# Joins of the 32-row inverses as products of two units, an fp32 second product in the small expert slots, and a new order table

## The chip, the core and the metric

The kernel runs on one core of a Trainium2 chip. The metric is the device time of one execution in microseconds (us). The core has five instruction queues that run side by side, each in its own order: PE (TensorE, the matrix products; its weight loads are counted apart as PEld), DVE (VectorE), ACT (ScalarE), POOL (GpSimd) and SP (SyncE, which here issues most transfers). An instruction that waits holds back everything behind it on its engine. A lower share of busy time on one engine says little by itself: the program has stages with different limits.

## What is computed

Three layers follow one another. The first is a delta-rule attention over 768 positions, for 32 units (4 batches of 8 heads, 48 wide):

```
for t in range(S):
    y[:, :, t] = einsum('bhd,bhde->bhe', q[:, :, t], state)
    v_old = einsum('bhde,bhd->bhe', state, k_n[:, :, t])
    state = state + beta * einsum('bhd,bhe->bhde', k_n[:, :, t], v - v_old)
```

Its output, 3072 rows of 384, goes into a layer of eight experts: each row picks the expert with the largest logit, and gets `gate * (relu(x @ w1[e]) @ w2[e])`, with 1024 hidden columns. The third layer is a gated network on all rows: `h = x @ w_in`, `g = h * sigmoid(h)`, `out = g @ w_out`, with 2048 hidden columns.

## The kernel before

**Attention.** Time is cut into six chunks t of 128 positions, each into two halves e of 64, each of these into two blocks of 32 rows; units come in two groups p of 16. Within 64 rows the recurrence is solved with the inverse of a triangular matrix. Its two diagonal 32-row blocks are inverted for all units at once on DVE: `to_lanes` transposes the Gram blocks (L354), `norms` and `scales` make the factors, `step` (L404, L410 and their neighbours) does 31 dependent elimination steps, and `spread` (L420) transposes the result back. From there PE joins the two 32-row inverses to one of 64 rows: `join` (px, L435) and `turn_upper` (pt, L444), each 32 products of 32x32 per chunk and group, both copied by ACT (`keep_join`), and `lower` (po, L456), 32 more. Then follow `weigh` (L472, L473), `update` (L489), `state` (L505), `read` (L519), the transposes of the output (L786) and the router's logits (L802, L810). State goes from half to half and from chunk to chunk, so that these run in a chain. The Gram products are L329, the eviction of the masked ones is L340.

**Router.** After chunks 2 and 5 a pass on DVE and PE (`rank`, `finish`, L837 to L1100) ranks the rows, places them in slots and makes the index lists. Group 0 has five small slots of 256 rows, from the first half of the positions; group 1 four regular slots of 512 rows.

**Small slots.** A slot goes through 8 hidden blocks c of 128 columns. For each, the weights are split into a rounded part and a remainder (ACT L1280, DVE L1283, both for w1 and for w2), the first product takes nine matmuls of 256 columns (L1226), ACT applies the relu and writes its rounded part (L1317), DVE writes the remainder (L1320), and the second product takes three matmuls of 384 columns for each of two row blocks (L1233 with out `po`). 5 slots of 8 blocks make 40 such steps.

**Regular slots and the third layer** do the same with 512 rows (L1226 with out `ph`, L1233 with out `poe`) and then with L1609 and L1626. While the expert slots run, DVE and ACT also unpack the third layer's 64-bit weights (L1498 to L1507).

**What sets the order.** Attention, router and small slots are one list of jobs. `Order.solve` gives each job a rank, from a table of numbers (`PLAN["rank"]`) and the planned cost of what depends on it, and builds one order for each engine from planned costs and dependences; `emit` writes the instructions in that order and puts dummy products (L683, "pulses") where PE would stand idle. Regular slots and third layer are written after that; the framework interleaves them.

Of the kernel before, what the change touches and what calls it, by code (L numbers as in the profile page):

```python
# [22 lines left out]
    one=3,  # L23
    rank=dict(
        kq=-239.1, qb=147.9, vs=127, kd=578.4, gr=546.9, gq=-202.8, Gc=-247.9, Kc=160.5, dg=-13.6, zero=-244.4,
        L=237.9, sc=-13.3, b2=167.7, ln=-189.8, va=362.8, st=401, sp=462.8, ga=-851.5, px=-535.6, pt=359.1, X=-283.4,
        T=525.1, po=127.7, o=117.8, w=565, wc=-96.5, up=-260.7, uc=474.7, ps=-321.1, sc2=659.4, py=-453, Y=991.4,
        out=-12.8, xt=177.8, xc=6.6, gt=105.9, wv1=989.6, wv2=209.6, wv4=522, wv5=388.1, one=278.9, kz=21.8,
        ask=332.1, gates=-98.2, val=689.8, fe=-28.1, xg=10, tr=535.4, th=-20.7, tl=267.6, s1h=609, s1l=111.9,
        s2h=215, s2l=68.5, fi=-316.7, rh=-579, rl=-41.6, se=540, ev=-129.8, ys=-3.2, kq0=-193.7, kq1=316, kq2=167.9,  # L30
        kq3=-402.6, kq4=441.9, kq5=-347.4, qb0=-385.7, qb1=-50.8, qb2=270.9, qb3=-148, qb4=236.9, qb5=-273.3,
        vs0=-154.6, vs1=389.7, vs2=-687.6, vs3=-414.5, vs4=516.3, vs5=-50, kd0=303.3, kd1=243.7, kd2=-122.1,
        kd3=237.6, kd4=27.8, kd5=11.9, gr0=311.6, gr1=332.7, gr2=448.3, gr3=593, gr4=92.4, gr5=585.6, gq0=110.8,
        gq1=142.8, gq2=257.1, gq3=485.4, gq4=128.6, gq5=8.9, Gc0=-90.3, Gc1=-187.1, Gc2=154.7, Gc3=494.8, Gc4=-106.5,
        Gc5=-286.8, Kc0=-237.1, Kc1=305.5, Kc2=207.8, Kc3=125.8, Kc4=-357.2, Kc5=-175.8, dg0=69.1, dg1=-574.4,
        dg2=-256.8, dg3=12, dg4=405.5, dg5=273, zero0=-54, zero1=-452.2, zero2=-377.7, zero3=-404.9, zero4=-41.9,
        zero5=-0.1, L0=-107.8, L1=120.6, L2=-181.8, L3=894.2, L4=387.6, L5=-525.1, sc0=449.4, sc1=-48.2, sc3=1031.7,
        sc4=-89.2, sc5=-268.2, b20=445.1, b21=-23.3, b22=-42.7, b23=-277.3, b24=-397.4, b25=-376.7, ln0=586.1,
        ln1=226.1, ln2=790.8, ln3=324.6, ln4=-521.3, ln5=-62.2, va0=516.2, va1=587.4, va2=604.8, va3=122.6,
        va4=-545.8, va5=680.5, st0=-244.5, st1=-650, st2=149.7, st3=-98.4, st4=109.9, st5=136.7, sp0=318.8, sp1=-397,  # L40
        sp2=-105, sp3=-270.1, sp4=332.3, sp5=246.3, ga0=664.7, ga1=135.6, ga2=281.1, ga3=-382.8, ga4=6.3, ga5=405.9,
        px0=-343.9, px1=122.6, px2=997.5, px3=512.2, px4=33.2, px5=250, pt0=820.3, pt1=-209.9, pt2=78.9, pt3=356.1,
        pt4=442, pt5=73.3, X0=103.8, X1=18.1, X2=-31, X3=135.3, X4=290.9, X5=28.6, T0=326.2, T1=6.3, T2=323.9,
        T3=178.2, T4=-45.6, T5=159.7, po0=92.1, po1=425, po2=-537.7, po3=4.5, po4=151.8, po5=1075.1, o0=5.3,
        o1=156.3, o2=487.5, o3=-9.3, o4=-4.3, o5=-172.3, w0=512.1, w1=543.7, w2=-613.9, w3=555.4, w4=-341.1, w5=17.4,
        wc0=-524.6, wc1=370.4, wc2=162.5, wc3=-396.4, wc4=132.4, wc5=43.8, up0=-144.5, up1=-17, up2=17.1, up3=404.2,
# [4 lines left out]
        out5=136.5, xt0=354.1, xt1=-244.1, xt2=-557.6, xt3=-21.9, xt4=-596.7, xt5=-3.3, xc0=137.4, xc1=587,  # L51
        xc2=-418.9, xc3=325.9, xc4=111.8, xc5=320.6, gt0=-54.3, gt1=1.7, gt2=74.9, gt3=48.9, gt4=135.4, gt5=-396.6,
    ), half=161.8,
    ex=146.6, n0=40, npre=40, tok=70,
)


# [1756 lines left out]
```

## Time and profile before

| | us |
|---|---|
| median of 3 runs | 971.99 |
| lowest and highest | 971.89, 973.62 |
| the profiled execution | 972.41 |
| its span on the core | 970.7 |

The span is what the trace covers; 1.7 us of the execution lie around it. The page gives PE as busy for 905.5 us (93%), weight loads 796.6 (82%), DVE 608.1 (63%), ACT 439.2 (45%), POOL 84.6 (9%). These are means over four stages that differ: attention up to about 296 us, small slots up to about 410, regular slots up to about 561, and the third layer. A table of the busy time of each engine by stage is the view to begin with. A busy PE is not a PE at its peak: dummy products count, and a matmul counts as busy while its pipeline fills. How far apart matmuls start tells what they cost in a dense run.

### The profile page before, as it was taken

How to read it: one execution, taken by the hardware profiler on the slowest of the kernel's cores; microseconds unless marked ns; L12 is line 12 of the kernel's file. 1: busy time of each engine (PE TensorE's matmuls, PEld its weight loads, DVE VectorE, ACT ScalarE, POOL GpSimd, SP SyncE). 2: the span in 40 equal slices, each digit the busy share in tenths (PEclk: the TensorE clock that was granted, in tenths of full speed). 3: DMA queues.
4: the chain of work that ended last, by engine and by line, in shares of the span. 5: the costliest groups of instructions: out<-in, count | busy, mean ns of one | idle time of the engine just before them, and what ended most of it. 6: DMA issues, size and time to landing. Idle time of an engine off the chain costs nothing. (4 is left out here: it accounts for less than half of the span.)

```text
span 970.7 us, 26047 instructions
## 1 busy us (share of the span) xinstructions
PE 905.5 (93%) x10897; PEld 796.6 (82%) x10897; DVE 608.1 (63%) x1724; ACT 439.2 (45%) x868; POOL 84.6 (9%) x85
## 2 busy tenths in 40 slices
PE   7779797898989888999998999999999999999997
PEld 4458686776879887788997999989999899999997
DVE  5999599679958999999643466533334333333332
ACT  4036373645866556756443454433323332332322
POOL 5000000000001213424211010000000000000000
PEclk8888897988979999999998999999999999999999
DMA  9942654445434533857541322001001000000000
GB/s 187 191 119 65 140 114 109 104 104 118 93 88 148 150 97 129 264 179 241 179 131 53 98 68 82 6 28 33 33 1 33 33 1 1 33 1 1 33 1 33
DMA packets 76273, 85.44 MB, mean 88 GB/s; under 512 B 38153, under 2 KB 62871, under 8 KB 76144
## 3 DMA queue, kind: packets, MB, share of 16 engines
q1 hardware_dynamic: 72816, 73.83, 28.8%
q0 software_dynamic: 3328, 9.83, 3.0%
q8 instruction: 88, 1.44, 0.7%
q14 instruction: 41, 0.34, 0.1%
HBM read 70.53 MB, written 14.55 MB: 88 GB/s over the span
## 5 line engine op out<-in xcount | busy, mean ns | idle before, releaser
L1626 PE MATMUL fpo<-o,fgh 128*128 128x384 f32 x768 | 184.3, 338 | 0.0
L1614 DVE TENSOR_TENSOR fy<-fph,fy 128x512 f32<-128x512 f32 x96 | 66.4, 692 | 161.4 <-ACT fy L1612 161.0
L1626 PEld LDWEIGHTS fpo<-o,fgh 128*128 128x128 f32 x768 | 139.3, 188 | 7.9 <-ACT fgh L1616 0.4
L1612 ACT ACTIVATE fy<-fph 128x512 f32<-128x512 f32 x96 | 57.5, 598 | 169.0 <-PE fph L1609 166.1
L1626 PE MATMUL fpo<-o,fgl 128*128 128x384 f32 x384 | 116.6, 338 | 0.0
L1609 PE MATMUL fph<-fxh,ih 128*128 128x512 f32 x288 | 113.7, 395 | 0.0
L1609 PE MATMUL fph<-fxl,ih 128*128 128x512 f32 x288 | 113.3, 394 | 0.0
L1618 DVE TENSOR_TENSOR fgl<-fy,fgh 128x512 fp32r<-128x512 f32 x96 | 66.5, 692 | 74.7 <-ACT fgh L1616 64.3
L1609 PE MATMUL fph<-fxh,il 128*128 128x512 f32 x288 | 113.2, 393 | 0.0
L1616 ACT CAST fgh<-fy 128x512 fp32r<-128x512 f32 x96 | 59.7, 622 | 80.6 <-DVE fy L1614 44.6
L1233 PE MATMUL poe<-wKT,pairs 128*128 128x384 f32 x384 | 76.5, 344 | 4.0 <-ACTq L1470 3.1
L1233 PEld LDWEIGHTS poe<-wKT,pairs 128*128 128x128 f32 x384 | 69.0, 192 | 7.4 <-ACTq L1470 3.4
L1626 PEld LDWEIGHTS fpo<-o,fgl 128*128 128x128 f32 x384 | 71.1, 188 | 0.5
L404 DVE TENSOR_TENSOR tmp<-A,L 128x126 f32<-128x126 f32 (+20 forms) x336 | 70.7, 252 | 0.8
L410 DVE TENSOR_TENSOR A<-A,tmp 128x126 f32<-128x126 f32 (+20 forms) x336 | 70.5, 251 | 0.0
L683 PE MATMUL po<-dense 128*128 128x512 bf16 x163 | 55.4, 457 | 14.4 <-DVE KB L340 5.3
L1233 PE MATMUL po<-wKT,hs 128*128 128x384 f32 x240 | 54.7, 355 | 11.1 <-DVE wKT L1283 6.8
L1609 PEld LDWEIGHTS fph<-fxl,ih 128*128 128x128 f32 x288 | 54.1, 188 | 10.5
L1609 PEld LDWEIGHTS fph<-fxh,il 128*128 128x128 f32 x288 | 54.1, 188 | 9.7
L1609 PEld LDWEIGHTS fph<-fxh,ih 128*128 128x128 f32 x288 | 54.1, 188 | 9.0
L1233 PEld LDWEIGHTS po<-wKT,hs 128*128 128x128 f32 x240 | 40.4, 193 | 16.2 <-DVE wKT L1283 8.8
L1226 PE MATMUL bank<-xh,wRH 128*128 128x256 f32 x240 | 51.5, 291 | 0.9 <-DVE wRH L1283 0.8
(435 smaller groups left out, 1594.5 us busy)
## 6 DMA issues: line engine op xcount, KB each, us to landing
raw<-in_moe_w_dram SPq DMA_DIRECT2D x72, 384.0 KB
ri<-in_moe_w_in_dram SPq DMA_DIRECT2D x12, 512.0 KB
ro<-in_moe_w_out_dram SPq DMA_DIRECT2D x16, 384.0 KB
vs<-in_vd_dram SPq DMA_DIRECT2D x12, 384.0 KB
KI<-in_kd_dram SPq DMA_DIRECT2D x24, 192.0 KB
Z<-vs SPq DMA_DIRECT2D x24, 192.0 KB
xs<-Y SPq DMA_DIRECT2D x48, 96.0 KB
fy<-ys SPq DMA_DIRECT2D x6, 768.0 KB
```

The source lines that it names most:

```text
L404: nc.vector.tensor_tensor(tv, r[:, :, j : j + 1].to_broadcast([128, c, n]), L[:, j : j + 1, j + 1 :].to_broadcast([128, c, n]), op=ALU.mult,)
L410: nc.vector.tensor_tensor(r[:, :, j + 1 :], r[:, :, j + 1 :], tv, op=ALU.add)
L683: return nc.tensor.matmul(room, dense, dense[:, None, :].to_broadcast([128, 4, 128]), start=True, stop=True).ins
L1226: self.nc.tensor.matmul(ph, a[:, k, :], b[:, k, :], start=(i == 0), stop=(i == 8))
L1233: self.mark = self.nc.tensor.matmul(o, a[:, cs], b, start=(c == 0 and i == 0), stop=(c == self.F - 1 and i == 2)).ins
L1609: nc.tensor.matmul(ph, a[:, k, fs], b[:, k, :], start=(n == 0), stop=(n == 8))
L1612: nc.scalar.activation(sg, ph, AF.Sigmoid)
L1614: nc.vector.tensor_tensor(gv, ph, sg, op=ALU.mult)
L1616: self.marks = [nc.scalar.copy(gh, gv).ins]
L1618: self.marks.append(nc.vector.tensor_tensor(gl, gv, gh, op=ALU.subtract).ins)
L1626: nc.tensor.matmul(po[c], a[:, rows], b, start=(f == 0 and i == 0), stop=(f == 15 and i == 2))
```

## The change

It has four parts.

**Joins.** `join`, `turn_upper` and `lower` take two neighbouring units in one product, with 64 columns in the left factor. px then holds all four 32x32 products of a pair; the copy of pt is written twice by ACT, each time multiplied by a column of zeros and ones (`halves`), so that the left factor of po is block-diagonal. 16 products stand where 32 stood. The buffer G is laid out so that the blocks to be inverted lie together.

**Small slots.** The second product reads the relu's output and w2 as plain fp32, one matmul per row block. The split of w2 and the remainder of the hidden rows are gone. The second product holds the raw w2 until it has read it.

**Buffers and dependences.** A and L have two buffers each, so a chunk's clearing and its transposition to lanes no longer wait for the chunk before; keys have five half-buffers in place of six. Steps of two chunks could be done together (`together`), for the chunks named in `pair`.

**Order.** Planned costs of PE jobs are changed, and all ranks in the table are new. Since the ranks are numbers, what they do is shown by the order below.

```diff
-    one=3,
+    one=3, pair=(),
     rank=dict(
-        kq=-239.1, qb=147.9, vs=127, kd=578.4, gr=546.9, gq=-202.8, Gc=-247.9, Kc=160.5, dg=-13.6, zero=-244.4,
+        kq=198.9, qb=242.4, vs=64.9, kd=1074.8, gr=178.8, gq=-206.4, Gc=265.8, Kc=-543.5, dg=116.5, zero=481.9,
...
-        for tag, w in (("KQ0", 3072), ("KQ1", 1024), ("RH", 1536), ("KT", 1536)):
+        for tag, w in (("KQ0", 3072), ("KQ1", 1024), ("RH", 1536)):
...
     def join(self, t, p):
+
         G = self.g(t, p)
-        px = self.st[t]["px", p] = self.bank([128, 8, 32], f"px{t}_{p}")
+        px = self.st[t]["px", p] = self.bank([128, 8, 2, 32], f"px{t}_{p}")
         for n in range(8):
-            for q in range(4):
-                e, w = divmod(q, 2)
-                r, u = slice(64 * e + 32, 64 * e + 64), 2 * n + w
-                self.nc.tensor.matmul(px[32 * q : 32 * q + 32, n], G[r, u, 0:32], G[r, u, 32:64], start=True, stop=True)
+            for e in range(2):
+                r, u = slice(64 * e + 32, 64 * e + 64), slice(2 * n, 2 * n + 2)
+                self.nc.tensor.matmul(px[64 * e : 64 * e + 64, n], G[r, 0, u].rearrange("p w c -> p (w c)"), G[r, 1, u], start=True, stop=True)
...
-        self.nc.scalar.copy(X, self.st[t]["p" + x, p])
+        if x == "x":
+            self.nc.scalar.copy(X, self.st[t]["px", p])
+        else:
+            for w in range(2):
+                self.nc.scalar.mul(X[:, :, w, :], self.st[t]["pt", p], self.halves[:, w : w + 1])
...
     def lower(self, t, p):
         X, T = self.st[t]["Xx", p], self.st[t]["Xt", p]
-        po = self.st[t]["po", p] = self.bank([128, 8, 32], f"po{t}_{p}")
+        po = self.st[t]["po", p] = self.bank([128, 8, 2, 32], f"po{t}_{p}")
         for n in range(8):
-            for q in range(4):
-                r = slice(32 * q, 32 * q + 32)
-                self.nc.tensor.matmul(po[r, n], T[r, n], X[r, n], start=True, stop=True)
+            for e in range(2):
+                r = slice(64 * e, 64 * e + 64)
+                self.nc.tensor.matmul(po[r, n], T[r, n].rearrange("p w c -> p (w c)"), X[r, n], start=True, stop=True)
...
-            add(("zero", t), "POOL", 1.0, lambda t=t: self.clear_inverses(t), [("sp", t - 1)])
+            add(("zero", t), "POOL", 1.0, lambda t=t: self.clear_inverses(t), [("sp", t - 2)])
             add(("L", t), "DVE", 1.9, lambda t=t: self.to_lanes(t),
-                [("dg", t, p, e) for p in range(2) for e in range(2)] + [("st", t - 1, 30)])
+                [("dg", t, p, e) for p in range(2) for e in range(2)] + [("st", self.together(max(t - 2, 0))[0], 30)] * (t > 1))
...
         def relu(s, c):
-            nc.scalar.activation(self.bufs["hh"][c % 2], v["ph", s, c], AF.Relu)
-
-        def rest_of(s, c):
-            nc.vector.scalar_tensor_tensor(
-                self.bufs["hl"][c % 2], v["ph", s, c], 0.0, self.bufs["hh"][c % 2], op0=ALU.max, op1=ALU.subtract
-            )
+            nc.scalar.activation(v["h"][c % 2], v["ph", s, c], AF.Relu)
 
         def second(s, c):
-            self.second(c, [x[:, 0:384] for x in self.po], *(self.bufs[x][c % 2] for x in ("hh", "hl", "h2", "l2")))
+            for b in range(2):
+                nc.tensor.matmul(
+                    self.po[b][:, 0:384], v["h"][c % 2][:, 128 * b : 128 * b + 128], self.raw(1, c),
+                    start=(c == 0), stop=(c == F - 1),
+                )
...
-                    old = [(f"s{part + 1}{x}", s - 1, c + k, 0) for x in "hl" for k in range(2)]
+                    old = [(x, s - 1, c + k, 0) for x in (("s1h", "s1l") if part == 0 else ("se",)) for k in range(2)]
```

What the new table does to the order is seen at three places. The first is DVE behind `spread` of the last chunk, before the change (L420 is the transposition, L871 to L882 and L837 to L841 are the router):

```order
L410 TENSOR_TENSOR A_4594<-A_4594,tmp_30_0_5333 128x16
L410 TENSOR_TENSOR A_4594<-A_4594,tmp_30_1_5335 128x15
L420 STREAM_TRANSPOSE G<-A_4594 128x32x32
L871 TENSOR_TENSOR rk_5371<-ranks,OH 128x64
L873 TENSOR_REDUCE r_0_5373<-rk_5371 128x8
L876 TENSOR_TENSOR ge_5375<-r_0_5373,k_131 128x192
L880 TENSOR_REDUCE pd<-ge_5375 128x8
L882 SCALAR_TENSOR_TENSOR pm<-pd,r_0_5373 128x8
L837 TENSOR_REDUCE mx_5445<-lg 128x4
L839 TENSOR_TENSOR eq_5447<-lg,mx_5445 128x32
```

Here the pass over group 0 follows the last `spread`. The same engine after the change, ahead of the steps of chunk 4 (L388 lengthens the values, L1124 and L1126 end the group's lists, L347 evicts Gram products, L361 goes to lanes, L399 and L403 begin the steps):

```order
L388 TENSOR_TENSOR vs_0_2777<-vs_0_2777,nt_3568 128x768
L1124 COPY gate_3948<-ranks 128x10
L1126 TENSOR_TENSOR gate_3948<-gate_3948,ranks 128x10 x2
L388 TENSOR_TENSOR vs_1_2936<-vs_1_2936,nt_3568 128x768
L347 TENSOR_TENSOR KB_109<-bank_128,amask 64x512 x2
L361 STREAM_TRANSPOSE L_3956<-G 128x1024
L399 TENSOR_TENSOR L_3461<-L_3461,b_4_3572 128x256
L403 SCALAR_TENSOR_TENSOR A_2419<-L_3461,A_2419 128x31
```

The whole pass over group 0, which stood behind the last `spread`, now stands ahead of the steps of chunk 4, and chunk 5's transposition to lanes (L361) ahead of them too. The second place is DVE at the end of chunk 4's steps and behind the last chunk's, after the change (L438 is `spread`, L1308 splits w1, L1335 a slot's rows):

```order
L422 TENSOR_TENSOR A_2419<-A_2419,tmp_27_1_4475 128x14x4
L1308 TENSOR_TENSOR wRH<-raw_4193,wRH 128x384
L416 TENSOR_TENSOR tmp_28_0_4490<-A_2419,L_3461 128x45
...
L438 STREAM_TRANSPOSE G<-A_2419 128x32x32
L1308 TENSOR_TENSOR wRH<-raw_4193,wRH 128x384
L373 RECIPROCAL rn_4528<-n_5_4014 128x32
...
L438 STREAM_TRANSPOSE G<-A_3272 128x32x32
L1308 TENSOR_TENSOR wRH<-raw_4193,wRH 128x384 x2
L388 TENSOR_TENSOR vs_0_3527<-vs_0_3527,nt_4533 128x768
```

Before the change no split of expert weights stood ahead of the last `spread`; now seven do. The third place is PE at the last chunk's joins, before the change (bank is a PSUM bank):

```order
L810 MATMUL bank_121<-ident,xT_0_5174 128x128
L435 MATMUL bank_122<-G 32x32 x32
L435 MATMUL bank_123<-G 32x32 x32
L444 MATMUL bank_119<-ident,G 32x32 x32
L444 MATMUL bank_120<-ident,G 32x32 x32
L683 LDWEIGHTS dense
L683 MATMUL po_170<-dense 128x512
```

and after it (L453 px, L461 pt, L480 po, L543 `read`, L1252 the first product of a small slot):

```order
L453 MATMUL bank_127<-G 64x64 x16
L461 MATMUL bank_128<-ident,G 64x32 x16
L453 MATMUL bank_124<-G 64x64 x16
L543 MATMUL bank_125<-Z_112,KB_108 64x48 x16
L480 MATMUL bank_126<-Xx_0_5184,Xt_0_5205 64x64 x16
L461 MATMUL bank_127<-ident,G 64x32 x16
L1252 MATMUL bank_128<-xh_4351,wRH 128x256
L1252 MATMUL bank_128<-xl_4352,wRH 128x256
```

A matmul of a small slot stands where a dummy product stood. Seven of the 40 steps of the small slots now stand ahead of the last chunk's px on PE, about ten more between the products of its tail. Dummy products fall from 163 to 103.

## Rows read from the trace of the kernel before

**Rows 1.** Busy time by stage: stretch, length, busy (count) by engine, granted clock, DMA.

```profile
core 0: us, PE busy (x) PEld busy (x) DVE busy (x) ACT busy (x) POOL busy (x), PEclk, DMA share, GB/s
138.90:178.20 39.30, 33.14 (x1029) 27.43 (x1026) 35.78 (x145) 16.76 (x37) 0.95 (x1) 0.83 0.46 102
178.20:231.80 53.60, 48.39 (x1519) 41.26 (x1515) 40.09 (x161) 33.07 (x70) 0.95 (x1) 0.90 0.52 118
231.80:262.00 30.20, 27.24 (x936) 22.01 (x925) 29.48 (x143) 20.12 (x44) 0.95 (x1) 0.89 0.41 94
262.00:286.00 24.00, 20.03 (x679) 15.61 (x681) 13.39 (x71) 13.58 (x30) 0.79 (x1) 0.79 0.36 73
296.00:410.40 114.40, 102.12 (x743) 95.40 (x744) 107.54 (x275) 70.77 (x161) 26.88 (x24) 0.97 0.46 147
410.40:560.60 150.20, 145.91 (x739) 131.28 (x739) 95.20 (x188) 75.80 (x152) 33.15 (x24) 0.98 0.46 147
560.60:970.70 410.10, 405.15 (x2059) 367.27 (x2057) 164.74 (x262) 137.05 (x234) 3.34 (x4) 1.00 0.07 25
```

**Rows 2.** The last two `spread`s on DVE, in the timeline: start, length, operation.

```profile
229.54 2.22 DVE L420 STREAM_TRANSPOSE G<-A 128x1024 f32<-128x1024 f32 x1
259.77 2.29 DVE L420 STREAM_TRANSPOSE G<-A 128x1024 f32<-128x1024 f32 x1
```

**Rows 3.** DVE's waits, 62 to 262 us: total, times, longest.

```profile
DVE KB L340 <- PE bank L329: 14.0, 8, 4.6
DVE rn L366 <- ACT n L360: 10.8, 2, 6.6
DVE lg L813 <- PE bank L810: 1.5, 1, 1.5
```

**Rows 4.** Waits of the router's pass over group 0, 262 to 296 us.

```profile
DVE rk L871 <- PE ranks L863: 7.5, 1, 7.5
DVE p1f L1077 <- PE ranks L1072: 1.5, 1, 1.5
```

**Rows 5.** Weight loads that waited for nothing shown, 62 to 296 us.

```profile
PEld bank L444 <- issue: 10.2, 4, 2.8
PEld bank L329 <- issue: 8.1, 7, 2.8
PEld bank L435 <- issue: 6.6, 5, 4.0
```

**Rows 6.** PE's timeline: 120 rows of px, 64 rows of `update`.

```profile
265.05 1.32 PE L435 MATMUL bank<-G 32*32 32x32 f32 x120
85.10 2.07 PE L489 MATMUL bank<-Z,KA 128*64 128x48 f32 x64
```

**Rows 7.** PE's timeline in a small slot: six second, nine first products, next second.

```profile
330.34 1.21 PE L1233 MATMUL po<-wKT,hs 128*128 128x384 f32 x6
331.38 0.28 PE L1226 MATMUL bank<-xh,wRH 128*128 128x256 f32 x1
...
332.45 0.52 PE L1233 MATMUL po<-wKT,hs 128*128 128x384 f32 x2
```

**Rows 8.** Chain that ended last: a run of twelve transposes of 128 fp32 columns.

```profile
549.07 1.31 PE fpt L1593 x12
```

**Rows 9.** Waits of PE and its weight loads in the small slots, 296 to 411 us.

```profile
PE po L1233 <- DVE wKT L1283: 6.8, 5, 3.0
PEld po L1233 <- DVE wKT L1283: 8.8, 7, 3.3
PEld po L1233 <- DVE hs L1320: 6.9, 9, 2.5
```

**Rows 10.** Groups by line, whole run: busy us, mean ns, idle before and releaser.

```profile
L1283 DVE TENSOR_TENSOR wKT<-raw,wKT 128x384 fp32r<-128x384 f32 x40 | 21.4, 550 | 0.9 <-ACT wKT L1280 0.8
L1320 DVE SCALAR_TENSOR_TENSOR hs<-bank,hs 128x256 fp32r<-128x256 f32 x40 | 16.6, 416 | 1.4 <-ACT hs L1317 1.3
L448 ACT COPY Xt<-bank 128x256 f32<-128x256 f32 x12 | 4.5, 373 | 15.0 <-PE bank L444 15.0
```

More of the change, by code (lines that the diff above doesn't have):

```diff
@@ L54 @@
-    ex=146.6, n0=40, npre=40, tok=70,
+        kq=198.9, qb=242.4, vs=64.9, kd=1074.8, gr=178.8, gq=-206.4, Gc=265.8, Kc=-543.5, dg=116.5, zero=481.9,
+        L=-45.2, sc=-154.7, b2=340.1, ln=213.1, va=184.7, st=-507.6, sp=-287.4, ga=-146.4, px=174.1, pt=-1057.9,
+        X=305.7, T=-753.7, po=227.7, o=-75.7, w=-47.4, wc=358.3, up=-972, uc=248.6, ps=313.7, sc2=440.7, py=-130,
+        Y=295.3, out=42.8, xt=584.3, xc=262.8, gt=-535.2, wv1=331.6, wv2=-1257.8, wv4=-528.6, wv5=1423.9, one=13,
+        kz=-116.7, ask=630.4, gates=494.4, val=-1272.9, fe=560.9, xg=-121.2, tr=351.3, th=-1084.9, tl=-543.8,
@@ L249, in __init__ @@
         nc.vector.memset(self.tiny, 1e-36)
+        self.halves = cp.tile([128, 2], F32, name="halves")
+        nc.vector.memset(self.halves, 0.0)
+        for q in range(4):
+            nc.vector.memset(self.halves[32 * q : 32 * q + 32, q % 2 : q % 2 + 1], 1.0)
         self.bl = cp.tile([128, T, 32], F32, name="bl")
-        self.G = cp.tile([128, 4, N, 64], F32, name="G")
+        self.G = cp.tile([128, 2, 2, U, 32], F32, name="G")
         self.st = [{} for _ in range(T)]
@@ L408, in step, with together, step_cost @@
             tmps.append(tv)
[L409 removed]
+        for (_, r), tv in zip(rows, tmps):
             nc.vector.tensor_tensor(r[:, :, j + 1 :], r[:, :, j + 1 :], tv, op=ALU.add)
     @staticmethod
[L413 to L414 removed]
+    def together(t):
+        return (t, t + 1) if t in PLAN["pair"] else (t - 1, t) if t - 1 in PLAN["pair"] else (t,)
+    def step_cost(self, t, j):
+        m, n = len(self.together(t)), 31 - j
+        x = m * 0.34 if j % 8 == 0 else 0.0
         if j < PLAN["one"]:
[L416 removed]
+            return x + 0.165 * (j + 1) * m
+        if m > 1:
+            return x + 2 * m * (0.068 + 0.00105 * n * (j + 1))
         return x + sum(2 * (0.068 + 0.00105 * n * c) for c in ((j + 2) // 2, (j + 1) // 2))
@@ L599, in plan @@
                         [("ln", t, p), ("up", t - 1, p, e), ("ps", t - 1, p, e), ("py", t - 1, p, e)], size=0.8)
-            for j in range(31):
-                add(("st", t, j), "DVE", self.step_cost(j), lambda t=t, j=j: self.step(t, j),
-                    [("b2", t) if j == 0 else ("st", t, j - 1)])
-            add(("sp", t), "DVE", 2.15, lambda t=t: self.spread(t), [("st", t, 30)])
+            ts = self.together(t)
+            if t == ts[-1]:
+                for j in range(31):
+                    add(("st", ts[0], j), "DVE", self.step_cost(t, j), lambda t=t, j=j: self.step(t, j),
+                        [("st", ts[0], j - 1)] if j else [("b2", x) for x in ts])
+                for x in ts:
+                    add(("sp", x), "DVE", 2.15, lambda x=x: self.spread(x), [("st", ts[0], 30)])
             for p in range(2):
@@ L677, in run @@
         nc, P = self.nc, self.pools
-        dense = P["ac"].tile([128, 128], BF16, name="dense")
-        nc.vector.memset(dense, 1.0)
+        dense = router.ones
         room = experts.po[1].rearrange("p (a b) -> p a b", b=128)
@@ L896, in rank @@
             ("choose", "DVE", 2.6, choose, ()), ("count", "PE", 0.1, count, ("choose",)),
-            ("exps", "ACT", 1.55, exps, ("choose",)), ("place", "DVE", 1.05, place, ("count",)),
+            ("exps", "ACT", 1.55, exps, ("choose",)), ("place", "DVE", 1.3, place, ("count",)),
             ("gates", "DVE", 1.6, gates, ("exps",)),
```

191 lines of the change are left out of this document (97 added, 94 removed).

## The prediction

> **What bounds the kernel now.** I began with busy time by stage. From 560.6 us to the end PE stands nearly full (405.2 of 410.1 us), and from 410.4 to 560.6 too (145.9 of 150.2) [rows 1]. The change leaves the work of these 560.3 us alone, so I carry them over whole and ask only when the last small slot ends; that is at 410.4 us now.
>
> Ahead of that two stages count. In the attention DVE leads: 35.8 of 39.3, 40.1 of 53.6, 29.5 of 30.2 us per chunk [rows 1]. PE looks as busy, but part of it is dummy products. The chain runs from `spread` to `spread`; the last one ends at 259.8 + 2.3 = 262.1 us [rows 2]. DVE's waits on the way sum to 14.0 + 10.8 + 1.5 = 26.3 us [rows 3]: Gram products that PE reaches late, and ACT's square roots. Behind the last `spread` the router's pass over group 0 takes 24.0 us, of which 7.5 + 1.5 = 9.0 are waits for PE [rows 1, 4]; the tail of the last chunk runs to about 296 us, and the small slots fill the 114.4 us behind it. There DVE is busy for 107.5 us [rows 1], and PE waits for DVE's remainders [rows 9].
>
> **The small slots, part by part.** DVE loses a split of w2 (550 ns) and a remainder of the hidden rows (416 ns) in each of 40 steps: 21.4 + 16.6 = 38.0 us [rows 10]. ACT loses as many copies. What is late next is PE. Six second products take 331.38 - 330.34 = 1.04 us, nine first ones 332.45 - 331.38 = 1.07 [rows 7]; a step is 2.11 us of PE now. After the change the second product is two fp32 matmuls of 384 columns. An fp32 matmul has two rows in the trace (64 rows of `update` for its two groups of 16 products), so a step has four rows of 384 columns. No row shows one of this width. The bounds: at the rate of the rounded rows (1.04/6 = 0.173 us) four are 0.69 us; at that of `update`, where 64 rows of 48 columns take 2.07 us [rows 6] and two of them may run side by side, 0.065 us per 48 columns, they are 2.07. Nearest are the transposes, fp32 of full height: twelve of 128 columns in 1.31 us [rows 8], 0.109 each, so 4 x 3 x 0.109 = 1.31 us. I take that: a step becomes 2.38 us, 0.27 dearer.
>
> The Trainium skill ("FP8 and Floating Point Precision", TensorE Precision Notes) speaks against this product: true fp32 takes four passes through the array, the reduced form one. Eight passes of 0.173 us would make 1.38 us, 0.07 more per step, and the sum for the 33 steps below 2.3 us longer.
>
> w2 in its raw form is now held until the second product, so its next load, on SP, waits for PE. The next use of a buffer is eight steps later, 19 us; at the stage's 147 GB/s [rows 1] a pair of blocks, 384 KB, moves in 2.7 us. I cost it at nothing; without that cover each load would cost its 2.7 us, and the loads queued behind it on SP would wait as well.
>
> **The joins.** 32 products become 16 of twice the width. 120 rows of px take 1.32 us, 0.7 us for a call of 64; 32 rows of the next wider kind take 1.0 [rows 6]. PE gains nothing in time: px and po lose 0.3 us a call, 24 calls, 7 us. Half of it lies under DVE, and the part behind the last `spread` is in the count below. ACT pays one more copy of pt, 373 ns [rows 10], twelve times, 4.5 us, and wider copies of px, some 2.5: about 0.6 us for each group on the tail. What the joins can give is instructions. Weight loads waited for "issue" 10.2 us at pt, 6.6 at px and 8.1 at the Gram products, 4.0 at the longest [rows 5]; the joins are 4608 rows of PE (1152 products, each two matmuls and two loads) and become half.
>
> The Trainium skill ("Runtime: NRT & Kernel Launch", Instruction fetch mechanics) holds that fetching is autonomous and mostly hidden; by it halving the rows would give nothing. These rows, if they are fetches, show that it isn't hidden here. In the sum I credit nothing for it by itself, only a share of DVE's waits, so by the skill's rule the forecast would lie up to the 16.3 us credited below higher, which is the first rival.
>
> **The order.** Now the last `spread`. The group's pass moves ahead of chunk 4's steps: it brings its 24.0 us less its waits, 15.0. Seven splits of w1 and two of a slot's rows move ahead too: 9 x 0.55 = 5.0 us. Against this stand the 26.3 us of waits. The order shows the Gram products ahead of the joins they used to follow, double buffers let L and the factors of the next chunk be made early, and the pass over the group fills the gap between chunks 3 and 4 where 6.6 us were lost. Some waits will stay, since PE, which is asked several times in that pass, is in order: I leave 10 us of the 26.3 + 9.0. The last `spread` then ends at 262.1 + 15.0 + 5.0 - 26.3 + 10 = 265.8 us.
>
> Behind it PE is the bound: DVE has 107.5 - 38.0 of the small slots' work left, less the 5.0 us above and 18 us that move behind (below): some 47 us. By the order PE then has 33 steps of 2.38 (78.5 us), 21 calls of the attention at about 1.0 [rows 6] (21), 54 transposes of 0.109 (5.9), router and gates (some 4), and eleven matmuls of the regular slots (2.6, each 512 of a block's 9216 columns): 112.0. One us passes until px begins, and 6 us I leave for waits in the chain, since ten steps now fill the tail. The last small slot ends at 265.8 + 1 + 112 + 6 = 384.8 us.
>
> Behind that stand the 560.3 us; less 2 for rows moved ahead, plus 2 since 32 of DVE's rows of unpacking (18 us) move from the small into the regular slots. DVE then has 95.2 + 18 = 113 us in a stretch of 150 [rows 1], most of it in the first 23 of 32 blocks; for those PE needs 23 x 410.1/96 = 98, at the third layer's rate of 96 blocks of the same size [rows 1]. So PE covers it. The span is 384.8 + 560.3 = 945.1, the execution 1.7 more, 946.8; the profiled one lies 0.4 above the median, so 946.4. I say 946.
>
> **Rivals.**
> The waits stay. The named 26.3 us go at one place and come back at another. `spread` ends at 282, the small slots at 401, the time is 962. For it: PE stays in order and full of attention products; most of DVE's waits are for them. Against it: the order places them earlier, and half the joins' rows are gone.
> All waits go. `spread` ends at 255.8, with 3 us lost in the tail the small slots at 371.8, and the time is 933. For it: DVE's rows fit without a gap. Against it: no stretch of this trace outside pure steps is so full.
> Slower. The group's pass, now in the chain, keeps its 9.0 us of waits for PE besides all the old ones, because count and sums stand on PE behind products that wait for ACT. `spread` ends at 291, and with small-slot products ahead of the tail's PE loses 12 us instead of 6: 291 + 1 + 112 + 12 = 416, the time is 978. It decides from the point where `spread` ends later than 289. For it: a single such wait cost 7.5 us [rows 4]. Against it: DVE reaches the pass after chunk 3's lanes, choosing and lengthening, when PE should be past the joins.
> The change doesn't do what it says. The list `pair` is empty, so the joint steps never occur and DVE's chain is no shorter. If the order gains just what it costs, the time is 972.
>
> **How the numbers follow.** Forecast (938 to 956) 0.52; the waits stay (956 to 969) 0.24; all waits go (930 to 938) 0.13; slower (974 to 990) 0.08; nothing 0.03. The fp32 product's bounds move the time by -20 us (0.62 x 33) and +25 us (0.76 x 33), and are unlikely that far. A measurement of this kernel tells about 0.2%, 2 us, from no change. Faster has 0.52 + 0.24 + 0.13, less 0.01 for the edge: 0.88; the same 0.04; slower 0.08. The range of 932 to 967 leaves out the lower part of the second best case, the top of the waits that stay, and the slower ones: about 2 in 10.
>
> **What would show it.** The last `spread` near 266 us; DVE's waits for L329 and the square roots near 10 us; px rows halved, and "issue" ahead of them small; PE dense from px of chunk 5 on; four rows per second product, about 0.33 us apart; the last small slot near 385 and 560 us behind it. I would be wrong if fp32 rows start over 0.4 us apart, if `spread` is later than 280, or if the regular slots show PE waiting for L1190's splits.

## The result and the profile after

The changed kernel takes 948.49 us (median of four runs, 943.76 to 952.2), before 971.94: a ratio of 0.9753, 95% interval 0.9706 to 0.98. Six later runs gave 945.71 and 0.9739 (0.9712 to 0.9766). The profiled execution took 947.22 us, span 945.5. The forecast was 946. Of the runs below, one each of `b_ss` (3738.67 us), `b_both` (1256.0) and `a_pulse` (3062.37) lies far above its fellows; the medians take it in, the ratios leave it out.

The stages of the kernel after, in the columns of [rows 1] (stretch, length, busy time and count by engine, granted clock, DMA):

```profile
core 0: us, PE busy (x) PEld busy (x) DVE busy (x) ACT busy (x) POOL busy (x), PEclk, DMA share, GB/s
...
169.80:236.40 66.60, 55.39 (x1198) 47.68 (x1197) 60.53 (x254) 38.16 (x80) 5.84 (x5) 0.90 0.54 147
236.40:262.60 26.20, 26.08 (x701) 22.56 (x699) 25.75 (x134) 20.64 (x46) 0.00 (x0) 1.00 0.23 45
262.60:296.00 33.40, 31.94 (x732) 28.14 (x733) 10.85 (x37) 26.75 (x60) 5.87 (x6) 1.00 0.51 134
296.00:386.00 90.00, 83.98 (x564) 64.82 (x564) 53.48 (x146) 38.52 (x90) 25.68 (x17) 0.98 0.39 120
386.00:535.00 149.00, 144.92 (x751) 130.48 (x750) 109.19 (x219) 79.16 (x159) 26.36 (x23) 0.99 0.51 167
```

The last `spread` stands where it stood in [rows 2], although a pass of the router and seven splits of the small slots have moved ahead of it. Behind it DVE is no longer full (53.48 of 90 us, against 107.54 of 114.4), and PE nearly is (83.98 of 90). Timeline of DVE after:

```profile
260.51 2.10 DVE L438 STREAM_TRANSPOSE G<-A 128x1024 f32<-128x1024 f32 x1
```

DVE's waits after, 62 to 262.6 us, in the columns of [rows 3]; those for ACT's square roots are gone:

```profile
DVE KB L347 <- PE bank L334: 6.0, 4, 2.8
DVE gate L1124 <- remote: 1.2, 1, 1.2
DVE wRH L1308 <- ACT wRH L1305: 0.8, 2, 0.6
```

Weight loads after that waited for nothing the profile shows, 62 to 296 us, in the columns of [rows 5] (L334 is the Gram product, L461 pt; px shows none):

```profile
PEld bank L334 <- issue: 2.5, 3, 1.6
...
PEld bank L461 <- issue: 0.4, 1, 0.4
```

A small-slot step after, in PE's timeline (start, length, operation, count): a second product, the first of nine first ones, the next second:

```profile
308.91 1.45 PE L1346 MATMUL po<-raw,hs 128*128 128x384 f32 x4
309.90 0.57 PE L1252 MATMUL bank<-xh,wRH 128*128 128x256 f32 x1
...
311.26 0.81 PE L1346 MATMUL po<-raw,hs 128*128 128x384 f32 x2
```

The second product ends inside the next product's line: that one lasts 0.57 us, against 0.28 in [rows 7]. So only the whole step, 2.35 us, is read from these lines.

So the time agrees with the sum. Whether it came from where the sum put it (order, DVE's freed time) the two traces can't say, since four parts changed at once.

### The profile page after: what moved, and what is told of

Same layout as the page of the kernel before. It is cut to its first block, busy times and chain, and to the rows that moved or that the text cites. A ratio compares the mean times of both kernels' runs of the same rounds, so it can differ in the third digit from the quotient of the medians.

```text
span 945.5 us, 23368 instructions
## 1 busy us (share of the span) xinstructions
PE 894.5 (95%) x9605; PEld 781.0 (83%) x9605; DVE 573.5 (61%) x1648; ACT 429.3 (45%) x842; POOL 83.7 (9%) x85
## 3 DMA queue, kind: packets, MB, share of 16 engines
q8 instruction: 78, 1.28, 0.6%
## 5 line engine op out<-in xcount | busy, mean ns | idle before, releaser
L1646 PE MATMUL fpo<-o,fq 128*128 128x384 f32 x384 | 116.6, 338 | 0.0
L1638 DVE TENSOR_TENSOR fq<-fy,fgh 128x512 fp32r<-128x512 f32 x96 | 66.4, 692 | 74.4 <-ACT fgh L1636 63.3
L1259 PE MATMUL poe<-w2s,pairs 128*128 128x384 f32 x384 | 77.5, 344 | 3.9 <-ACTq L1490 3.2
L1259 PEld LDWEIGHTS poe<-w2s,pairs 128*128 128x128 f32 x384 | 69.2, 191 | 8.0 <-ACTq L1490 3.5
L1646 PEld LDWEIGHTS fpo<-o,fq 128*128 128x128 f32 x384 | 71.1, 188 | 0.5
L1252 PE MATMUL bank<-xh,wRH 128*128 128x256 f32 x240 | 61.3, 332 | 6.6 <-DVE wRH L1308 6.0
L1346 PE MATMUL po<-raw,hs 128*128 128x384 f32 x160 | 60.4, 501 | 0.0
L1629 PE MATMUL fph<-fq,ih 128*128 128x512 f32 x144 | 56.9, 395 | 0.0
L1629 PE MATMUL fph<-fxl,ih 128*128 128x512 f32 x144 | 56.5, 392 | 0.0
L1252 PEld LDWEIGHTS bank<-xh,wRH 128*128 128x128 f32 x240 | 41.6, 199 | 11.8 <-DVE wRH L1308 6.8
L709 PE MATMUL po<-ones 128*128 128x512 bf16 x103 | 32.9, 432 | 14.1 <-DVE KB L347 6.8
```

The lines of the kernel that those rows point to most:

```text
L709: return nc.tensor.matmul(room, dense, dense[:, None, :].to_broadcast([128, 4, 128]), start=True, stop=True).ins
L1252: self.nc.tensor.matmul(ph, a[:, k, :], b[:, k, :], start=(i == 0), stop=(i == 8))
L1259: self.mark = self.nc.tensor.matmul(o, a[:, cs], b, start=(c == 0 and i == 0), stop=(c == self.F - 1 and i == 2)).ins
L1346: nc.tensor.matmul(self.po[b][:, 0:384], v["h"][c % 2][:, 128 * b : 128 * b + 128], self.raw(1, c), start=(c == 0), stop=(c == F - 1),)
L1629: nc.tensor.matmul(ph, a[:, k, fs], b[:, k, :], start=(n == 0), stop=(n == 8))
L1638: self.marks.append(nc.vector.tensor_tensor(gl, gv, gh, op=ALU.subtract).ins)
```

## The experiments

The theory at first: the order takes the waits out of DVE's chain, the fp32 product takes DVE's work out of the small slots. All twelve runs at a glance. Median time, ratio to runs of before beside it (95% interval), start of the last `spread` and of the last small slot's eviction; then two sums over rows of the waits view from 62 us to the end of the last `spread`: issue on weight loads, and all waits of DVE.

```
               us       ratio (95%)              spread  evict   issue  DVE waits
before         971.94                             259.8  411.1   31.2   26.7
after          948.49   0.9753 (0.9706 .. 0.9800) 260.5  386.1    7.5    8.0
b_ss           965.91   0.9977 (0.9951 .. 1.0003) 257.5  408.7   29.9   24.3
b_join         945.97   0.9790 (0.9740 .. 0.9841) 234.5  380.6    4.7    1.0
b_both         947.07   0.9722 (0.9689 .. 0.9756) 240.2  388.8    6.9    6.7
b_mix2         952.33   0.9803 (0.9782 .. 0.9824) 239.9  393.5    4.5    6.5
b_pad         1024.34   1.0584 (1.0526 .. 1.0642) 286.6  459.8    4.6   53.0
b_newrank     1001.42   1.0348 (1.0314 .. 1.0381) 294.4  413.9   25.4   34.6
a_oldrank     1019.21   1.0556 (1.0506 .. 1.0606) 243.8  393.6    6.6   11.2
a_join32       966.17   0.9959 (0.9940 .. 0.9978) 275.8  404.8   26.1   23.0
a_dve          964.48   0.9931 (0.9907 .. 0.9956) 264.1  405.5    6.7    6.7
a_again        945.71   0.9739 (0.9712 .. 0.9766) 260.2  384.2    7.3    7.7
a_pulse        945.42   0.9736 (0.9708 .. 0.9764) 257.8  381.7    6.0    4.2
b_both_pulse   945.07   0.9725 (0.9701 .. 0.9750) 238.2  387.2    7.4    4.7
```

**`b_ss`: the fp32 product alone.**

```diff
-            self.second(c, [x[:, 0:384] for x in self.po], *(self.bufs[x][c % 2] for x in ("hh", "hl", "h2", "l2")))
+            for b in range(2):
+                nc.tensor.matmul(self.po[b][:, 0:384], v["h"][c % 2][:, 128 * b : 128 * b + 128], self.raw(1, c), ...)
```

> The kernel before with one part alone: the fp32 second product of the small slots (its splits of w2 and the remainder of the hidden rows gone from ACT and DVE), under before's own table. My theory: the gain of the change is made of two shares, DVE's work taken out of the small slots and the waits taken out of the chain from spread to spread. This kernel has the first share alone. The last spread stays near 262 us. Behind about 296 us PE becomes the bound: 40 steps of 2.35 us (94) and some 10 us of other products, so the last small slot ends at about 400 instead of 410.4 and the time is about 962. Rival A, the fp32 product carries the whole gain: 948. Rival B, the table carries the whole gain and the dearer product only costs PE 0.24 us in each of 40 steps: 972 to 982.

0.9977, an interval that takes in 1: less than expected, if anything. From the last `spread` to the last eviction it is 151.2 us (408.7 - 257.5), before 151.3: DVE's 38 us are gone, and the stretch is no shorter. That PE's four fp32 rows take their place fits, but is not shown by itself. Rival A falls.

**`b_join`: the joins alone.** `join`, `turn_upper`, `lower` and the layout of G as in after, with the planned costs, dependences and small buffers that go with them; the table is before's. Since planned costs enter the order, some evictions of Gram products and logits stand a few places earlier or later among DVE's steps than before.

```diff
-                self.nc.tensor.matmul(px[32 * q : 32 * q + 32, n], G[r, u, 0:32], G[r, u, 32:64], start=True, stop=True)
+                self.nc.tensor.matmul(px[64 * e : 64 * e + 64, n], G[r, 0, u].rearrange("p w c -> p (w c)"), G[r, 1, u], start=True, stop=True)
```

> The kernel before with the joins alone: products of two units, half as many, and the new layout of G they need, under before's own table. My theory: the idle time that weight loads show ahead of pt and px as issue (10.2 + 6.6 us in before) falls below 3 us, but most of it lay beside DVE's steps, so the last spread moves only by the part of DVE's 14.0 us of waits for Gram products that stands behind the joins, 3 to 5 us; ACT's wider copies take back 1 to 2; the time is 967 to 971. Rival C, instruction fetching was the limit of the attention and the halved rows carry the gain: last spread at 250, time about 955. Rival D, fetching is hidden anyway: issue waits as before, 972.

0.979, with the old table: this is nearly all of the change, and the first theory falls. The last `spread` starts 25.3 us earlier (in the profiled run, the fastest of four: 941.76 to 950.22). DVE's waits from 62 us to its end come to one row:

```profile
DVE rn L372 <- ACT n L366: 1.0, 1, 1.0
```

Its weight loads that wait for issue, 62 to 296 us (L333 is the Gram product, L441 px):

```profile
PEld bank L333 <- issue: 1.5, 4, 0.4
...
PEld bank L441 <- issue: 0.8, 3, 0.4
```

Why half as many products gain 25 us when a call of them is longer is seen in PE's timeline of before, behind the 120 rows of px in [rows 6]:

```profile
267.77 0.23 PE L435 MATMUL bank<-G 32*32 32x32 f32 x5 [1.40 <-issue]
267.80 0.23 PE L444 MATMUL bank<-ident,G 32*32 32x32 f32 x4
267.83 0.20 PE L435 MATMUL bank<-G 32*32 32x32 f32 x3
267.85 1.39 PE L444 MATMUL bank<-ident,G 32*32 32x32 f32 x116
271.50 0.33 PE L444 MATMUL bank<-ident,G 32*32 32x32 f32 x8 [2.26 <-issue]
271.76 1.46 PE L683 MATMUL po<-dense 128*128 128x512 bf16 x3
273.02 0.23 PE L862 MATMUL ranks<-OH,tri 128*128 128x32 bf16 x1
273.09 0.19 PE L863 MATMUL ranks<-ca,ones 128*128 128x32 bf16 x1
273.21 1.80 PE L456 MATMUL bank<-Xx,Xt 32*32 32x32 f32 x115
275.33 0.43 PE L456 MATMUL bank<-Xx,Xt 32*32 32x32 f32 x13 [0.31 <-issue]
```

From one stop to the next PE runs 5 + 4 + 3 + 116 = 128 matmul rows, then 8 + 3 + 1 + 1 + 115 = 128 again. Each has a weight load, so that is 256 instructions. The instruction queue of the page of before:

```profile
q8 instruction: 88, 1.44, 0.7%
```

1.44 MB in 88 packets is 16.4 KB a packet. By the page PE has 2 x 10,897 rows, which would make 66 bytes a row and 248 rows a packet: by these counts nearly all of the queue is PE's, and a packet holds one such run. Cut into half microseconds, the view of DMA shows q8 packets of before in the stretches that begin at 260.5, 265.0, 268.5, 272.5 and 276.5. PE got through a packet of narrow joins in about 1.5 us and then stood until the next came: 267.77 to 271.50 and on to 275.33 are 3.73 and 3.83 us a packet, 29 to 30 ns a matmul row, whatever the products need. Nowhere between 58 and 150 us are two packets nearer than about 3 us. In finer windows the packets start at 265.1, 268.95, 272.6 and 276.55 us: each starts 1.1 to 1.2 us after PE has gone on with the one before, and PE goes on 2.5 to 2.7 us after its start. So in this stretch the packets come one after the other, and PE, through with one in about 1.5 us, waits out the rest. Two px calls of the new kind, in PE's timeline of `b_join`:

```profile
63.73 1.91 PE L441 MATMUL bank<-G 32*64 32x64 f32 x58 [0.67 <-DVE G L426]
65.42 0.24 PE L449 MATMUL bank<-ident,G 32*64 32x32 f32 x2
65.47 0.22 PE L441 MATMUL bank<-G 32*64 32x64 f32 x2
```

Here 58 rows take 1.7 us, also 29 ns a row, and nothing stops. So, if the rate of that stretch holds ahead of the last `spread` too, a narrow call of 64 rows costs 64 x 29.5 = 1.9 us of supply, a wide one of 32 rows 0.9. Thirty calls (five chunks, two groups, three joins) stand ahead of the last `spread`: by this estimate 30 x 1.0 = 30 us of PE, of which 25.3 arrive there, and 15.3 under after's order (275.8 - 260.5, next run).

**`a_join32`: after, with the joins alone put back.** Planned costs, table and buffers stay after's, so the order does too: up to the last `spread` DVE's instructions are the same, one for one. This run tells the joins from the order.

```diff
-                self.nc.tensor.matmul(px[64 * e : 64 * e + 64, n], G[r, 0, u].rearrange("p w c -> p (w c)"), G[r, 1, u], start=True, stop=True)
+                self.nc.tensor.matmul(px[32 * q : 32 * q + 32, n], G[r, 0, u], G[r, 1, u], start=True, stop=True)
```

> The kernel after, its table, costs, double buffers and fp32 product kept, with the joins alone put back: 32 products of 32x32 per chunk and group instead of 16 of twice the width, one copy of pt, in the new layout of G. New theory, after the joins alone gave 0.979: the gain of the change is the joins, because PE's queue of small instructions was held up ahead of them (issue) and the Gram products behind it came late to DVE. Then issue waits of 15 us or more come back on PE between 62 us and the last spread, DVE waits 10 us or more for Gram products, the last spread ends at 275 to 290 and the time is 962 to 980. Old theory, order and freed DVE time carry the gain: 945 to 953, since the calls of 32 small products are no longer on PE (0.56 us a call in before) than the new ones (0.88).

0.9959: the same from the other side. The new order with all else new, but narrow joins, is 0.4% faster than before. Its DVE waits for Gram products from 62 us to the last `spread`:

```profile
DVE KB L347 <- PE bank L334: 17.4, 7, 5.3
```

In the same stretch its weight loads wait for issue again (L462 is pt, L474 po):

```profile
PEld bank L462 <- issue: 6.5, 4, 2.2
...
PEld bank L334 <- issue: 4.6, 4, 1.8
PEld bank L474 <- issue: 4.4, 4, 2.4
```

**`b_pad`: is it the number of instructions or the narrow shape?** `b_join`, with a product of one column ahead of each real one, overwritten by it (shown for px; pt and po likewise).

```diff
+                self.nc.tensor.matmul(px[64 * e : 64 * e + 64, n, 0, 0:1], G[r, 0, u].rearrange("p w c -> p (w c)"), G[r, 1, 2 * n, 0:1], start=True, stop=True)
                 self.nc.tensor.matmul(px[64 * e : 64 * e + 64, n], G[r, 0, u]...
```

> The kernel before with the joins in products of two units, its own table, and ahead of each of the 576 new products one more of the same left factor and a single column, whose result the real product overwrites. So PE's rows are as many as in before (about 10,900 for matmuls and as many loads, 1152 each more than with the joins alone), while the shape of the real products is the new one. Theory F, the 32-row products held PE up because its instructions did not arrive as fast as it got through them: the number counts, not the shape. Then issue waits of 10 us or more come back between 62 us and the last spread, DVE waits 8 us or more for Gram products, the last spread ends at 250 to 265 and the time is 958 to 972. Theory G, the narrow shape itself was slow (32 rows by 32 columns in a quarter of the array): the padding costs PE at most 0.3 to 0.5 us a call, beside DVE's steps, the issue waits stay below 4 us, the last spread ends at 236 to 243 and the time is 944 to 952.

1.0584, which neither theory allowed, so it doesn't tell them apart. I had taken the padding for nearly free. PE's timeline, in the 64-column form and at full clock:

```profile
63.99 0.28 PE L441 MATMUL bank<-G 32*64 32x1 f32 x4
64.08 0.36 PE L442 MATMUL bank<-G 32*64 32x64 f32 x4
64.23 0.28 PE L441 MATMUL bank<-G 32*64 32x1 f32 x4
```

Eight rows take 64.23 - 63.99 = 0.24 us, 30 ns a row: a row of one column costs what a row of 64 does. At that pace PE hardly outruns its packets, and few issue waits are left (4.6 us). A padded call has 64 rows again, 1.9 us like a narrow one, which would put the last `spread` back at before's 259.8 us; it starts at 286.6. The rest fits the clock. From 62 to 200 us the granted clock is 0.75, in before 0.85, and at the lower of its two levels (1.2 GHz, against 2.4) such rows take longer:

```profile
66.49 0.41 PE L441 MATMUL bank<-G 32*64 32x1 f32 x4
66.92 0.41 PE L441 MATMUL bank<-G 32*64 32x1 f32 x4
```

Between these starts lie eight rows, in 0.43 us, 54 ns a row. Of the 1920 join rows ahead of the last `spread` 1076 start at that level; at 24 ns more each that makes 26 us, an estimate, against 26.8 to be explained. DVE waits 53.0 us:

```profile
DVE KB L346 <- PE bank L333: 17.0, 3, 10.7
DVE rn L372 <- ACT n L366: 16.0, 1, 16.0
DVE lg L830 <- PE bank L827: 15.8, 1, 15.8
```

What it does show: in the attention PE's time is not slack. Rows put into the joins come back at the end, and at the lower level nearly twice. It agrees with 1.9 us for 64 rows; but since wide rows need 29 to 30 ns by themselves, it can't say whether number or shape sets that price for the narrow ones.

**`b_newrank` and `a_oldrank`: the tables exchanged.** Only `rank`, `half` and `ex` are swapped. (After's table has no numbers for the splits of w2 and the remainder of the hidden rows, which `b_newrank` still has; they count as 0 there.)

> The kernel before with after's table of numbers (and its half and ex) and nothing else. My theory: the table is fitted to small slots in which DVE has 38 us less to do; with the splits back, the steps pulled ahead of the last spread and into the tail put 0.97 us each into DVE's chain, and the old joins stand ahead of the Gram products again: slower than before, 975 to 990, last spread later than 275. Rival B (the table alone carries the gain): 948 to 955.

> The kernel after with before's table of numbers (and its half and ex) put back; joins, fp32 products, double buffers and the planner's new costs stay. My theory: the shares that need no table stay (DVE's freed time, about 10 us), the share that comes from the order (the group's pass in the gap between chunks 3 and 4, steps of the small slots pulled into the tail) is lost: 955 to 965. Rival A (the parts carry it, not the table): 948. Rival B (the table carries the whole gain): 972 or more.

Both are slower than either parent: 3.5% and 5.6% above before. That is more than I gave for `b_newrank`; for `a_oldrank` only rival B left room for it (972 or more), and `b_join` and `b_both` speak against that rival. They say that a table belongs to the jobs and costs that it was found with, not what it is worth. In `a_oldrank` the last `spread` is early (243.8) and the last small slot at 393.6, but the router's pass over group 1 now lies behind the small slots, and from the last eviction to the end it is 623.7 us (1017.3 - 393.6), in after 559.4 (945.5 - 386.1). The stretch behind them, in the table of stages:

```profile
394.00:450.00 56.00, 16.93 (x321) 14.11 (x317) 37.36 (x112) 14.10 (x28) 6.47 (x8) 0.66 0.39 131
```

And the longest of PE's waits there, from 394 to 620 us:

```profile
PE ranks L1097 <- DVE scratch L1066: 18.4, 1, 18.4
```

**`b_both`: all new work under the old table.** The two edits of `b_ss` and `b_join` together; the table as before.

> The kernel before, its own table, with the joins and the fp32 product together: all parts of the change that alter work, none that alter the order. New theory: the last spread ends near 236 us as with the joins alone; in the small slots behind it DVE falls from 104 to about 70 of 111 us but PE rises from 96 to 107 (40 steps, 0.27 us each), so nothing is won there: 940 to 948, the same as the joins alone within 0.5%. Rival A, the fp32 product has a share of its own: the last small slot 10 us earlier, 930 to 936.

0.9722, beside 0.9753 and 0.9739 for after: the new order and the double buffers bring nothing that these runs can tell. Nor is `b_both` told apart from `b_join` (0.979); their intervals overlap. The two orders share the span out differently: in `b_both` the last `spread` starts at 240.2 and the last eviction 148.6 us behind it, in after 260.5 and 125.6.

**`b_mix2`: fp32 in every second block.** `b_join` with `plain(s, c) = c % 2 == 1`.

> The kernel before, its own table, with the joins, and the fp32 product in every second hidden block only (20 of 40 steps; the others keep the split). New theory: with all steps split DVE is the bound of the small slots (104 of 111 us), with none PE is (107); half and half DVE has 85 and PE 101, so the last small slot ends 4 to 8 us earlier than with the joins alone, 934 to 940. If what decides is the chain of waits between ACT, DVE and PE within a step and not the sums, nothing is won: 942 to 948.

0.9803: nothing won; 952.33 us lies above both ranges, but the ratio is not told apart from that of `b_join` (0.979). From 300 to 394 us DVE is busy for 88.0 of 94 us and PE for 81.6, so that neither sum is balanced as I had worked it out; PE waits for the remainders of w2, w1 and the hidden rows:

```profile
PE po L1244 <- DVE wKT L1295: 4.6, 4, 2.1
PE bank L1237 <- DVE wRH L1295: 3.0, 1, 3.0
PE po L1244 <- DVE hs L1332: 2.4, 2, 1.7
```

**`a_dve`: DVE's work put back as idle work.** In after, 40 times:

```diff
             nc.scalar.activation(v["h"][c % 2], v["ph", s, c], AF.Relu)
+            nc.vector.scalar_tensor_tensor(v["dump"][:, 0:256], v["ph", s, c], 0.0, v["h"][c % 2], op0=ALU.max, op1=ALU.subtract)
...
+            nc.vector.tensor_tensor(v["dump"], self.raw(1, c), self.raw(1, c), op=ALU.subtract)
```

> The kernel after with DVE's two instructions per small-slot step put back as idle work: a subtraction of 384 columns and a remainder of 256 columns into a scratch that nobody reads, 40 times, some 0.97 us a step, PE's order unchanged. New theory: behind the last spread DVE is idle for about 47 of 123 us, so only the 7 steps ahead of it, 6.8 us, and a few waits where DVE is in order reach the end: 953 to 960. Rival A, DVE's freed time is what shortens the small slots: 33 steps of 0.97 us more behind the spread besides, 32 + 7 us: 980 or more. Rival E, nothing of it counts: 948.

0.9931, 16 to 19 us slower than after: between the two. The last `spread` is 3.6 us later, the rest is lost behind it. There was room on DVE in sum, but not in its queue: the idle remainder waits for ACT's relu, the splits of w1 stand behind it, and PE waits for these, where it waited 6.0 us in after. Of DVE's waits in `a_dve`, 240 to 406 us, the one row that after lacks (two larger ones, for ACT's part of w1 and for xh, are there in after too):

```profile
DVE hs L1344 <- ACT hs L1343: 10.4, 8, 2.2
```

And of PE's, 262 to 406 us:

```profile
PE bank L1252 <- DVE wRH L1309: 12.6, 9, 3.9
```

So in the new order DVE's freed time is worth up to 16 to 19 us, before what the fp32 product costs PE, 0.24 us a step. In the old order the whole part, with that cost in it, was worth 2 to 7 (2 by `b_ss`, 7 by `b_both` less `b_join`, neither told from nothing). That the new order relies on a free DVE fits this, but the 16 us are not DVE's queue alone: PE's waits for w1's splits grow by 6.6 us, and the granted clock from 262 to 300 us is 0.78 where after has 1.00. (The table was not made for the extra work, which counts against this run.)

**`a_again`, `a_pulse`, `b_both_pulse`: the scatter of after, and a faster version.** The two latter have denser dummy products up to 62 planned us.

```diff
-                x = max(at + 0.02, j["start"] - 9.0)
+                x = max(at + 0.02, j["start"] - (14.0 if at < 62 else 9.0))
-                    x += 0.43
+                    x += 0.25 if x < 62 else 0.43
```

> The kernel after, unchanged, beside the two below on the same chip. It scattered by 0.9% where before scattered by 0.2%. Theory K: its PE is so dense in the attention that spells at half the granted clock, which come in some runs and not in others, reach the end; then time and mean clock go together, some 1 us of time for 0.0017 of clock as in the four runs seen (943.8 at 0.980, 952.2 at 0.966), and the median is 945 to 951. Theory N, the scatter has nothing to do with the clock: no such relation in the runs.

> The kernel after with denser dummy products in the first 62 planned us alone: one each 0.25 us instead of 0.43 where PE is planned idle, and up to 14 us ahead of the next job instead of 9; 91 more of them. Theory K, the half-clock spell at 62 to 78 us (0.66 in the profiled run of after) follows idle PE ahead of it and costs time: the granted clock there goes to 0.95 or above, the runs lie at 942 to 945 and scatter by less than 0.5%. Theory N: the spell comes from something else, or is hidden beside DVE's chain: the clock there as before, or better without any gain in time, 946 to 950. If the dummies get in the way of jobs that come early, 950 or more.

> The kernel before, its own table, with the joins and the fp32 product together as measured (0.9722), and the same denser dummy products in the first 62 planned us. If the new table is worth nothing net and the clock is what scatters, this is the fastest of the three: 936 to 942, the last spread at 234 to 237 as with the joins alone in its undisturbed run. If the dummies bring nothing: 943 to 948. If the table of after is worth something that the clock hid: after's dense version is faster than this one by 3 us or more.

All three are at 945 us. In `a_again` time and mean clock go together as in the first four runs (942.91 us at 0.979, 948.36 at 0.969: 1 us for 0.0018), so the scatter goes with the clock, as theory K has it; which of the two leads is not shown. The granted clock from 62 to 78 us (between the levels of 1.2 and 2.4 GHz) was 0.66 again in `a_again`, its row in the table of stages:

```profile
62.00:78.00 16.00, 14.61 (x305) 13.54 (x306) 15.47 (x63) 8.46 (x17) 0.95 (x1) 0.66 0.26 67
```

In `a_pulse` it was 1.00:

```profile
62.00:78.00 16.00, 15.81 (x441) 13.17 (x441) 15.42 (x58) 11.22 (x24) 0.95 (x1) 1.00 0.43 118
```

The medians are the same all the same: denser dummies went with full clock in that stretch, as theory K has it, but the time that K put on the spell did not come back (945.42 us, scatter 0.6%). Spells between 170 and 235 us stay (0.90 and 0.89 in `a_pulse`). `b_both_pulse` is no faster than `b_both`, and within 1 us of `a_pulse`, so the clock hid no worth of the new table there. No version measured here beats after by more than the intervals.

## Why the prediction was right

The time was right, and most steps of the sum were. The step on the joins was wrong, and with it the reason for the largest credit. That the total came out is in part luck: the last `spread` ended 3.2 us early, what stands behind it took 4.0 us longer, and the two nearly cancel.

- **What is carried over.** 560.3 us behind the last small slot; measured 945.5 - 385.6 = 559.9, from the start of the last row of the last second product, which is what 410.4 was in before. The moved unpacking is covered by PE, as said.
- **The fp32 second product.** Taken at 1.31 us, a step at 2.38. Measured 311.26 - 308.91 = 2.35, with 1.07 for nine first products 1.28; the cost is 0.24 us a step. The Trainium skill ("FP8 and Floating Point Precision", TensorE Precision Notes) has true fp32 take four passes; by that rule it was 1.38, and the trace lies 7% below. That it speaks against the product is borne out in the old order: `b_ss` gained nothing that counts.
- **DVE's 38 us.** Gone, and PE is what is late next, as said. That the cover is thin was not said: `a_dve` suggests that the order within DVE's queue counts, and not only the sum.
- **The joins.** Here the working failed: "PE gains nothing in time: px and po lose 0.3 us a call" and "In the sum I credit nothing for it by itself, only a share of DVE's waits". I priced a narrow call by its rows in a dense burst (0.7 us) and took the issue waits for something apart. They are the price of the same rows: packets of 128 matmul rows came 3.7 to 3.8 us apart in [rows 5]'s stretch, so a narrow call costs 1.9 us and a wide one 0.9. By this estimate the term should have been a gain of 30 calls x 1.0 us on PE ahead of the last `spread`, of which 25.3 (`b_join`) and 15.3 (`a_join32`) were measured there, not a loss of 7. The Trainium skill ("Runtime: NRT & Kernel Launch", Instruction fetch mechanics) has instructions come in blocks of 256, and the cost of passing from one to the next mostly hidden. The first agrees with the 128 matmuls and 128 loads between two stops. By the second the waits stay and the time is 962. There the traces disagree: 31.2 us of issue waits with 10,897 matmul rows, 4.7 in `b_join` with 9743.
- **The waits.** 10 us were to stay of DVE's 26.3 and the pass's 9.0; 8.0 stayed, and the last `spread` ended at 262.6 against 265.8. Right in size by luck, wrong in cause: I gave it to the order ("The order shows the Gram products ahead of the joins they used to follow, double buffers"). The joins alone take them to 1.0 us under the old order, and without them 23.0 us are there under the new one.
- **What moved ahead, and the tail.** The pass and the splits were to bring 20.0 us ahead of the last `spread`; DVE's busy time from 62 us to its end grew by 17.1 (187.0 against 169.9). Behind the last `spread` 123.0 us (385.6 - 262.6) against 119, PE's waits for w1's splits 6.0 against 6.
- **The order as a whole.** It moves those 17 us of DVE's work ahead of the last `spread` and takes 23.0 us from what follows in comparison with `b_both` (148.6 to 125.6). The two cancel, but for what the intervals hide.
- **The rivals.** "The waits stay" (962) is what the kernel does without the joins: `a_join32` is at 966. "Slower" would have needed the waits of the pass, of which 1.2 us were left. "All waits go" had against it that no stretch was so full; after kept 8.0 us, but `b_join` is at 1.0.

**What stays open.** How much of the 25 us is supply and how much the spells below full clock is not separated. `b_join`, `b_mix2` and `b_both` have the same order up to the last `spread`, which starts at 234.5, 239.9 and 240.2; the first shows no spell below full clock from 62 to 200 us, the others one each. That puts one spell at some 5 us. The granted clock from 62 to 260 us is 0.87 in before and 0.99 in `b_join`, which at two levels is some 51 us against 4 at the lower one: spells of that price could carry as much as the supply. That the joins bring the gain is shown from both sides; how it divides between these two ways is not. `b_pad`, meant to tell number from shape, told neither. What would make packets come faster was not tried.

## What to carry to other kernels

Count the instructions of a run of small products, not only their durations: where issue waits come after equal numbers of rows, divide the time between two stops by that number, and price every row at that rate. Merging neighbours into block-diagonal products then pays even where each product gets longer and half of its result is thrown away. And when a change has four parts, test the parts both ways, added to the old and taken from the new: here swapping the tables alone would have given the order a wrong share.

## What the hardware showed that I had not expected

- PE's instructions come in packets of 16.4 KB, by the counts above one for 128 matmuls and their loads; in the joins PE stood still after exactly 128 rows, twice running, and got a packet each 3.7 to 3.8 us.
- Rows of 32x32 products start 11 to 12 ns apart (120 rows in 1.32 us, 116 in 1.39), of products with 64-column left factors 29 to 30 ns, with one column on the right as with 64; in a stretch at 1.2 GHz 54 ns. A padding product is no cheaper than a real one.
- The granted clock falls in some executions of one order and not in others: 62 to 78 us is at 1.00 in `b_join` and at 0.63 in `b_mix2`, whose PE had the same instructions in the same order until then. The row of `b_join` in the table of stages:

```profile
62.00:78.00 16.00, 15.33 (x484) 14.12 (x484) 15.43 (x66) 13.39 (x28) 0.95 (x1) 1.00 0.27 77
```

That of `b_mix2`:

```profile
62.00:78.00 16.00, 15.37 (x333) 14.39 (x333) 15.43 (x66) 9.23 (x19) 0.95 (x1) 0.63 0.19 45
```
